# Attention and two gated layers on one core: v loaded head by head, block-diagonal q made ahead of k's high part, early weight pieces moved to other tiles

## The chip, the cores and the metric

The kernel runs on one core of one Trainium2 chip. The metric is the device time of one execution in microseconds (us); the median of several executions is compared. The engines are named as in the profile: PE (TensorE, matmul) with its weight loads PEld, ACT (ScalarE), DVE (VectorE), POOL (GpSimd) and SP (SyncE, which here only issues DMAs).

## The reference

Three stages follow each other. The attention has 4 batches of 8 heads, 1152 keys and head size 64; each pair of neighbouring queries is averaged first, so there are 576 queries a head.

```python
q_pool = q.reshape(B, H, S // 2, 2, D).mean(axis=3)
scores = scale * np.matmul(q_pool, k.transpose(0, 1, 3, 2))
scores = scores - np.max(scores, axis=-1, keepdims=True)
attn = np.exp(scores)
attn = attn / (np.sum(attn, axis=-1, keepdims=True) + 1e-09)
out = np.matmul(attn, v)
...
x = out.transpose(0, 2, 1, 3).reshape(B * S, H * D)      # 2304 x 512
h = x @ w_in;  x = (h - np.tanh(h)) @ w_out              # layer 1, d_ff 2048
h = x @ w2_in; x = (h / (1.0 + np.exp(-1.702 * h))) @ w2_out   # layer 2
```

The weights arrive as 64-bit floats, which the kernel reads as pairs of 32-bit integers.

## The kernel before

**Precision.** Every matmul operand is split into a high part that the matmul takes exactly (`qh`, `kh`, `vh`, `ph`) and a low part that is the rest (`ql`, `kl`, `vl`, `pl`), and a product is three matmuls (high by high, high by low, low by high). So each tensor costs a cast and a subtraction besides the matmuls: casts mostly on ACT, subtractions on DVE or POOL.

**Pairs and steps.** Two heads make a pair (16 pairs, numbered 0 to 15 here). A pair has 18 steps, i = 0 to 17: nine key blocks of 128 for each of its two heads. One step of the loop over `g` does, in this order: the scores of step g in two halves (four matmuls, L319 and L320), the exponentials `pf` and `ph` of each half on ACT (L321, L323), every second step a row-maximum tile for the pair that is next (`max_tile`: three matmuls L281 and a reduction on DVE, L284), `pl = pf - ph` of step g-1 (`rest`, L332; on POOL where i of that step is 2, 5, 8 or 11, else on DVE), and the six matmuls of probabilities by values of step g-3 (`pv`, L348). The scores have three PSUM buffers of half a step, the maximum tile has one. When a head's nine blocks are through, ACT copies the two halves of its sum out of PSUM (`u`, L354), which comes at i = 2 and i = 11.

**What is prepared for later pairs.** Each engine runs its instructions in program order, and the order is written by hand. `plan` gives, for the pair p+2 (or p+3), the step at which its pieces are emitted during pair p: `prep_qh` (ACT), `prep_kh` in two halves (ACT, L252), `prep_bdq` (ACT, two instructions, L247: q of the two heads laid out block-diagonally, the weights of the maximum tiles), `prep_ql` (DVE), `prep_kl` (POOL, L262), and the loads of q, k and v by SP. For the next pair n = p+1, `stack` at i = 2 and i = 13 issues six copies each from SP that lay out a head's operands (`a`, `q`), `max_rows` at i = 13 issues four more with the maxima (`q<-tt`), and `prep_v` at i = 3 and i = 12 makes `vh` and `vl` of one head on POOL (L301, L304).

**v.** `load_v` brings v of a whole pair, both heads, into the one buffer `vr` (576 KB) at i = 14. That buffer is last read by `prep_v` of the second head at i = 12, and the new contents are first read by `prep_v` at i = 3 of the next pair.

**Weights.** A weight piece is loaded (`ld`, L109, into one of two `raw` buffers) and then converted in three stages: stage 0 (ACT L122; DVE L123, L127), stage 1 (DVE L134, L138) and the split into high and low part (ACT L145, POOL L146). Layer 1's first eight pieces are spread over attention by the table `when`: kind ("i" for w_in, "o" for w_out), number, and then (pair relative to 16, step) of the load and of the three stages. Stages that the table does not name go into the first windows of layer 1. `split_x` at steps 13 to 16 of pair 15 splits the first block of the layer's input (cast on ACT L101, subtraction L102).

**Layers.** A window n of layer 1 or 2 is `h_part` (24 matmuls L552), the gate on ACT and DVE (`gate`), and two windows later `y_part` (L639). In layer 1 the gate's DVE instructions are L588, L594, L603, L606 and L608; jobs of weight conversion are run between L594 and L603.

Of the kernel before, what the change touches and what calls it, by code (L numbers as in the profile page):

```python
# [7 lines left out]
F32 = mybir.dt.float32  # L8
# [20 lines left out]
def tile_pooled_attention_two_moe(  # L29
# [14 lines left out]
    D = 64  # L44
# [141 lines left out]
    def attention(ctx: ExitStack):  # L186
# [34 lines left out]
        def load_v(p):  # L221
            vraw[p] = ap.tile([128, 2, KT, D], F32, tag="vr", name="vr")
            nc.sync.dma_start(out=vraw[p], in_=v[p // NPB, p % NPB])
# [19 lines left out]
        def prep_bdq(p):  # L243
            qs = pairs[p]["qs"]
            for s in range(2):
                r = slice(64 * s, 64 * s + 64)
                nc.scalar.activation(  # L247
                    bdqs[p % 2][r, :, r], qs[r, :].rearrange("p (j c) -> p j c", j=QJ), AF.Copy)
# [49 lines left out]
        def prep_v(p, s):  # L298
            vr = vraw[p]
            vh, vl = vt[(2 * p + s) % 3]  # L300
            nc.gpsimd.tensor_scalar(  # L301
                out=vh[:, :, 0:D], in0=vr[:, s], scalar1=1.0, scalar2=1.0,
                op0=ALU.mult, op1=ALU.mult)
            nc.gpsimd.tensor_tensor(  # L304
                vl[:, :, 0:D], vr[:, s], f32(vh[:, :, 0:D]), op=ALU.subtract)
# [84 lines left out]
        def normalise(p):  # L390
# [31 lines left out]
        for c in range(NKC):  # L422
            early.setdefault((NPAIR - 1, 13 + c), []).append(
                lambda c=c: split_x(0, [c], nc.gpsimd))
# [15 lines left out]
        load_v(0)  # L440
# [6 lines left out]
        with tc.tile_pool(name="ps_first", bufs=2, space=PSUM) as ps_first:  # L447
            for j in range(QJ):
                max_tile(0, j, ps_first)
                if j == 4:  # L450
                    prep_qh(1)
                    prep_kh(1, 0)
                    prep_kh(1, 1)
                    prep_bdq(1)
                    fill(2)
# [7 lines left out]
        load_v(1)  # L463
# [7 lines left out]
        for n in range(1, NPAIR):  # L471
# [4 lines left out]
            (2, 2): [(prep_qh,)], (2, 4): [(prep_kh, 0)], (2, 7): [(prep_kh, 1)],  # L476
            (2, 10): [(prep_bdq,)], (2, 14): [(prep_ql,), (load_v,)],
# [264 lines left out]
```

## Time and profile before

| | us |
|---|---|
| three runs | 1396.39, 1400.29, 1401.53 |
| median | 1400.29 |
| the profiled execution, its own time | 1398.61 |
| its span, first to last instruction | 1396.8 |
| PE busy in the span | 1316.1 (94%) |
| DVE busy | 1048.5 (75%) |
| ACT busy | 843.7 (60%) |
| POOL busy | 439.5 (31%) |

The span is 1.8 us shorter than the execution's own time. Busy shares are averages over attention and the two layers, which use the engines differently, so they do not tell what a step waits for; that is read from the timeline and the waits of the stretch in question.

### The profile page before, as it was taken

To read this page: it belongs to the slowest core of one execution; us is meant where nothing else is said; L and a number is where in the kernel's file an instruction comes from. 1 tells how busy PE (TensorE), PEld (TensorE's weight loads), DVE (VectorE), ACT (ScalarE), POOL (GpSimd) and SP (SyncE) were. 2 spreads that over 40 slices of the span, in tenths; PEclk is the share of its full clock that TensorE was granted. 3 is DMA by queue.
4 is the path that set the end of the run, shared out by engine and by line. 5 is a ranking of instruction groups with operands and counts; after the bars stand their busy time and mean duration, and the time that the engine had idled before them with its cause. 6 is when DMAs were issued, how large, how long until landed. Compare 5 with 4: busy or idle time off the path is not lost.

```text
span 1396.8 us, 20802 instructions
## 1 busy us (share of the span) xinstructions
PE 1316.1 (94%) x7632; PEld 1243.2 (89%) x7632; DVE 1048.5 (75%) x1230; ACT 843.7 (60%) x1885; POOL 439.5 (31%) x314
## 2 busy tenths in 40 slices
PE   4999999999999988899999999999999999999998
PEld 3999889998989887899899889899999999999997
DVE  5888887889898878898888888889963554645433
ACT  2798878988888776677656555656643422222211
POOL 6254444444445456233322332332310110110000
PEclk9899999999999999999999999999999999999999
DMA  7466666565667452111110110111110110110011
GB/s 191 123 173 165 154 146 164 148 162 141 165 149 174 102 122 83 58 46 31 46 46 31 42 35 31 46 46 31 46 60 31 46 46 31 52 39 31 24 46 68
DMA packets 44037, 117.70 MB, mean 84 GB/s; under 512 B 11936, under 2 KB 11936, under 8 KB 43936
## 3 DMA queue, kind: packets, MB, share of 16 engines
q1 hardware_dynamic: 43900, 116.38, 31.4%
q8 instruction: 60, 0.98, 0.3%
q14 instruction: 41, 0.34, 0.1%
q10 hardware_dynamic: 36, 0.00, 0.0%
HBM read 66.58 MB, written 4.79 MB: 51 GB/s over the span
## 4 chain that ended last, share of the span: by engine, by line
PE 47%; DVE 28%; ACT 9%; issue 5%; DMA 4%; POOL 3%; SPq 3%; DVEq 0%; POOLq 0%; ACTq 0%
PE y L639 14%; PE h L552 14%; PE pv L348 9%; PE mx L281 4%; DVE gg L606 3%; DVE gg L603 3%; PE sc L319 3%; DVE gg L608 3%; PE sc L320 3%; DVE d L594 3%; DMA vr<-in_v_dram 2%; ACT d L587 2%; DVE wt L123 2%; DVE wt L127 2%; DVE gg L588 2%
## 5 line engine op out<-in xcount | busy, mean ns | idle before, releaser
L321 ACT ACTIVATE pf<-sc 128x288 f32<-128x288 f32 x576 | 243.7, 425 | 75.8 <-PE sc L320 71.9
L323 ACT ACTIVATE ph<-sc 128x288 fp32r<-128x288 f32 x564 | 242.2, 429 | 0.0
L284 DVE TENSOR_REDUCE mt<-mx 128x1 fp32r<-128x1152 f32 x144 | 194.1, 1350 | 57.7 <-PE mx L281 57.4
L332 DVE TENSOR_TENSOR pl<-pf,ph 128x576 fp32r<-128x576 f32 x224 | 208.6, 953 | 6.9 <-ACT ph L323 6.0
L564 POOL TENSOR_TENSOR g<-gg,g 128x768 fp32r<-128x768 f32 x48 | 89.0, 1853 | 300.3 <-ACT g L562 281.0
L319 PE MATMUL sc<-q,a 128*128 128x288 f32 x576 | 169.2, 305 | 9.3 <-ACT pf L321 3.7
L320 PE MATMUL sc<-q,a 65*128 65x288 f32 x576 | 167.3, 303 | 2.6 <-DMA q<-tt 2.6
L612 ACT ACTIVATE a<-h 128x768 f32<-128x768 f32 x48 | 39.0, 812 | 214.5 <-PE h L552 214.5
L348 PE MATMUL pv<-pl,vh 128*128 128x288 f32 x576 | 140.3, 307 | 15.0 <-POOL pl L332 12.2
L652 DVE TENSOR_TENSOR xb<-xb,y 128x384 f32<-128x384 f32 (+1 forms) x126 | 73.0, 606 | 93.2 <-PE y L639 93.2
L348 PE MATMUL pv<-ph,vh 128*128 128x288 f32 x576 | 136.7, 301 | 3.9 <-ACT u L354 3.8
L348 PE MATMUL pv<-ph,vl 128*128 128x288 f32 x576 | 134.5, 297 | 0.0
L281 PE MATMUL mx<-kh,bdq 128*128 128x384 f32 x432 | 108.4, 362 | 24.4 <-DVE mt L284 16.8
L552 PE MATMUL h<-hl,w 128*128 128x384 f32 x720 | 130.5, 335 | 0.0
L332 POOL TENSOR_TENSOR pl<-pf,ph 128x576 fp32r<-128x576 f32 x64 | 107.3, 1676 | 65.3 <-ACT ph L323 55.3
L552 PEld LDWEIGHTS h<-hl,w 128*128 128x128 f32 x720 | 126.4, 188 | 1.2
L319 PEld LDWEIGHTS sc<-q,a 128*128 128x128 f32 x576 | 112.7, 196 | 16.2 <-ACT ph L323 9.9
L605 ACT ACTIVATE a<-u 128x768 f32<-128x768 f32 x48 | 40.7, 848 | 131.8 <-DVE gg L603 131.8
L348 PEld LDWEIGHTS pv<-pl,vh 128*128 128x128 f32 x576 | 96.6, 192 | 20.8 <-POOL pl L332 15.3
L320 PEld LDWEIGHTS sc<-q,a 65*128 65x128 f32 x576 | 111.6, 194 | 3.1 <-issue 3.1
L615 DVE TENSOR_TENSOR gg<-h,a 128x768 f32<-128x768 f32 x48 | 45.8, 955 | 84.8 <-ACT a L612 84.8
L348 PEld LDWEIGHTS pv<-ph,vh 128*128 128x128 f32 x576 | 102.5, 192 | 7.1 <-ACT u L354 6.9
(114 smaller groups left out, 2954.4 us busy)
## 6 DMA issues: line engine op xcount, KB each, us to landing
a<-kh SPq DMA_DIRECT2D x64, 288.0 KB
raw<-in_moe_w_in_dram SPq DMA_DIRECT2D x32, 512.0 KB
raw<-in_moe_w_out_dram SPq DMA_DIRECT2D x32, 512.0 KB
qr<-in_q_dram SPq DMA_DIRECT2D x16, 576.0 KB
kr<-in_k_dram SPq DMA_DIRECT2D x16, 576.0 KB
vr<-in_v_dram SPq DMA_DIRECT2D x16, 576.0 KB
q<-qh SPq DMA_DIRECT2D x64, 144.0 KB
a<-kl SPq DMA_DIRECT2D x32, 288.0 KB
```

What stands on the lines that cost most here:

```text
L281: nc.tensor.matmul(mx[:, a, 0:384], bdqs[p % 2][:, j, :], d["kh"][:, a * 384:(a + 1) * 384], start=True, stop=True)
L284: nc.vector.tensor_reduce(d["mt"][:, j:j + 1], mx[:, :, 0:384], AX.XY, ALU.max, negate=True)
L319: nc.tensor.matmul(sc, a1[:, ks], q2[:, xs], start=True, stop=False)
L320: nc.tensor.matmul(sc, a2[:, ks], q3[:, xs], start=False, stop=True)
L321: nc.scalar.activation(pf[:, xs], sc, AF.Exp, scale=SCALE)
L323: nc.scalar.activation(ph[:, xs], sc, AF.Exp, scale=SCALE)
L332: eng.tensor_tensor(pl, pf, f32(ph[:]), op=ALU.subtract)
L348: nc.tensor.matmul(accs[hd][x], w[:, t, :], r[:, x * HB:(x + 1) * HB], start=(t == 0 and n == 0), stop=(t == KT - 1 and n == 2))
L552: nc.tensor.matmul(hb[:, j, 0:TB], wi[:, c, w, :], x[r][c], start=(k == 0), stop=(k == 3 * NKC - 1))
L564: eng.tensor_tensor(gt[:, :, 1, :], g, f32(gt[:, :, 0, :]), op=ALU.subtract)
L639: nc.tensor.matmul(ys[m][:, 0:w], lhsT, rhs, start=(fp == 0 and k == 0), stop=(fp == 1 and k == 5))
L652: nc.vector.tensor_add(dst, dst, ys[m][:, 0:w])
```

## The change

v gets a buffer for each head of a pair (`vr0`, `vr1`, half the size each), with a load for each: the first head's at i = 6, the second's at i = 14. The block-diagonal q is emitted as two separate jobs at i = 4 and i = 5, and the halves of k's high part move from i = 4 and 7 to i = 6 and 8; `prep_ql` moves from i = 14 to i = 15. In the table `when` the loads and stages of the eight weight pieces get other steps, and all stages of piece ("o", 3) now stand in attention, so that none of them is left for layer 1. Two of the four subtractions of `split_x` for the first block go from POOL to DVE.

```diff
--- before.py
+++ after.py
@@ -218,9 +218,9 @@
             kraw[p] = ap.tile([128, S], F32, tag="kr", name="kr", bufs=2)
             nc.sync.dma_start(out=kraw[p], in_=k[p // NPB, p % NPB])
 
-        def load_v(p):
-            vraw[p] = ap.tile([128, 2, KT, D], F32, tag="vr", name="vr")
-            nc.sync.dma_start(out=vraw[p], in_=v[p // NPB, p % NPB])
+        def load_v(p, s):
+            vraw[p, s] = ap.tile([128, KT, D], F32, tag=f"vr{s}", name=f"vr{s}")
+            nc.sync.dma_start(out=vraw[p, s], in_=v[p // NPB, p % NPB][:, s])
 
         def prep_qs(p, eng=None):
             pairs[p] = dict(
@@ -240,12 +240,11 @@
             d = pairs[p]
             nc.vector.tensor_sub(d["ql"], d["qs"], f32(d["qh"][:]))
 
-        def prep_bdq(p):
-            qs = pairs[p]["qs"]
-            for s in range(2):
-                r = slice(64 * s, 64 * s + 64)
-                nc.scalar.activation(
-                    bdqs[p % 2][r, :, r], qs[r, :].rearrange("p (j c) -> p j c", j=QJ), AF.Copy)
+        def prep_bdq(p, s):
+            r = slice(64 * s, 64 * s + 64)
+            nc.scalar.activation(
+                bdqs[p % 2][r, :, r],
+                pairs[p]["qs"][r, :].rearrange("p (j c) -> p j c", j=QJ), AF.Copy)
 
         def prep_kh(p, x):
             xs = slice(x * SP, (x + 1) * SP)
@@ -296,13 +295,13 @@
                     queues[a].dma_start(out=row[:, :, a, :], in_=f32(tt[g:g + QJ, :]))
 
         def prep_v(p, s):
-            vr = vraw[p]
+            vr = vraw.pop((p, s))
             vh, vl = vt[(2 * p + s) % 3]
             nc.gpsimd.tensor_scalar(
-                out=vh[:, :, 0:D], in0=vr[:, s], scalar1=1.0, scalar2=1.0,
+                out=vh[:, :, 0:D], in0=vr, scalar1=1.0, scalar2=1.0,
                 op0=ALU.mult, op1=ALU.mult)
             nc.gpsimd.tensor_tensor(
-                vl[:, :, 0:D], vr[:, s], f32(vh[:, :, 0:D]), op=ALU.subtract)
+                vl[:, :, 0:D], vr, f32(vh[:, :, 0:D]), op=ALU.subtract)
 
         probs, accs, halves = {}, {}, {}
 
@@ -404,14 +403,14 @@
         pool_cast = range(NPAIR * NS - NS + 2, NPAIR * NS, 3)
         early = {}
         when = (
-            ("i", 0, (-8, 6), (-7, 5), (-7, 8), (-7, 16)),
-            ("i", 1, (-6, 6), (-5, 5), (-5, 8), (-5, 16)),
-            ("o", 0, (-4, 6), (-3, 5), (-3, 8), (-3, 16)),
-            ("i", 2, (-2, 2), (-2, 8), (-2, 11), (-2, 16)),
-            ("i", 3, (-2, 14), (-1, 4), (-1, 5), (-1, 7)),
-            ("o", 1, (-1, 0), (-1, 7), (-1, 8), (-1, 10)),
-            ("o", 2, (-1, 6), (-1, 11), (-1, 12), (-1, 14)),
-            ("o", 3, (-1, 9)),
+            ("i", 0, (-8, 6), (-7, 6), (-7, 14), (-6, 7)),
+            ("i", 1, (-6, 6), (-5, 6), (-5, 14), (-4, 7)),
+            ("o", 0, (-4, 6), (-3, 6), (-3, 14), (-2, 5)),
+            ("i", 2, (-2, 0), (-2, 6), (-2, 12), (-2, 14)),
+            ("i", 3, (-2, 4), (-2, 13), (-2, 15), (-2, 17)),
+            ("o", 1, (-2, 14), (-1, 1), (-1, 3), (-1, 5)),
+            ("o", 2, (-2, 16), (-1, 4), (-1, 6), (-1, 9)),
+            ("o", 3, (-1, 4), (-1, 8), (-1, 10), (-1, 12)),
         )
         ahead = []
         for kind, f, *steps in when:
@@ -421,7 +420,7 @@
             ahead += jobs[len(steps):]
         for c in range(NKC):
             early.setdefault((NPAIR - 1, 13 + c), []).append(
-                lambda c=c: split_x(0, [c], nc.gpsimd))
+                lambda c=c: split_x(0, [c], nc.gpsimd if c < 2 else nc.vector))
 
         load_q(0)
         load_k(0)
@@ -437,7 +436,8 @@
         prep_ql(0)
         load_q(1)
         load_k(1)
-        load_v(0)
+        load_v(0, 0)
+        load_v(0, 1)
         prep_kl(0, 0)
         prep_kl(0, 1)
         stack(0, 0)
...
         plan = {
-            (2, 2): [(prep_qh,)], (2, 4): [(prep_kh, 0)], (2, 7): [(prep_kh, 1)],
-            (2, 10): [(prep_bdq,)], (2, 14): [(prep_ql,), (load_v,)],
+            (2, 2): [(prep_qh,)], (2, 4): [(prep_bdq, 0)], (2, 5): [(prep_bdq, 1)],
+            (2, 6): [(prep_kh, 0), (load_v, 0)], (2, 8): [(prep_kh, 1)],
+            (2, 14): [(load_v, 1)], (2, 15): [(prep_ql,)],
             (2, 16): [(prep_kl, 0)], (2, 17): [(prep_kl, 1)], (3, 5): [(load_q,)],
             (3, 7): [(load_k,)], (3, 16): [(prep_qs,)],
         }
```

(In the part left out the two loads of v and the two jobs of block-diagonal q of the first pairs are written one after the other, where one call stood.)

**Block-diagonal q on ACT.** The rows show ACT in pair 1, around step 10 as it was: `bdq` after the last `ph` of step 10, then step 11's exponentials and the copies `u` of the finished head.

```order
L323 ACTIVATE ph<-sc 128x288
L247 ACTIVATE bdq_82<-qs 64x9x64 x2
L321 ACTIVATE pf<-sc 128x288
L323 ACTIVATE ph<-sc 128x288
L321 ACTIVATE pf<-sc 128x288
L323 ACTIVATE ph<-sc 128x288
L354 ACTIVATE u<-pv_786 128x288
L354 ACTIVATE u<-pv_787 128x288
```

In the change the same two instructions (now L245) stand in the same pair behind steps 4 and 5, and the first half of `kh` (now L251) behind step 6:

```order
L322 ACTIVATE ph<-sc 128x288
L245 ACTIVATE bdq_82<-qs 64x9x64
L320 ACTIVATE pf<-sc 128x288
L322 ACTIVATE ph<-sc 128x288
L320 ACTIVATE pf<-sc 128x288
L322 ACTIVATE ph<-sc 128x288
L245 ACTIVATE bdq_82<-qs 64x9x64
L320 ACTIVATE pf<-sc 128x288
L322 ACTIVATE ph<-sc 128x288
L320 ACTIVATE pf<-sc 128x288
L322 ACTIVATE ph<-sc 128x288
L251 ACTIVATE kh<-kr 128x576
```

Between step 10 and the copies `u` nothing but the exponentials is left on ACT.

**Loads of v in SP's queue.** The rows show SP around the turn from pair 7 to pair 8 as it was: the end of a `stack`, the load of v of a pair, the next `stack`, the sums `s`, then the loads of q, of weight piece ("i", 0) (`raw`) and of k.

```order
L275 DMA q_2_96<-ql 64x576
L223 DMA vr<-in_v_dram 128x1152
L270 DMA a_0_72<-kh 64x1152
...
L275 DMA q_0_90<-ql 64x576
L362 DMA s_4112<-u 64x1x9
L364 DMA s_4112<-u 64x1x9
L215 DMA qr<-in_q_dram 128x1152
L109 DMA raw<-in_moe_w_in_dram 128x1024
L219 DMA kr<-in_k_dram 128x1152
```

The same place in the change:

```order
L274 DMA q_2_96<-ql 64x576
L223 DMA vr_3926<-in_v_dram 128x576
L269 DMA a_0_72<-kh 64x1152
...
L274 DMA q_0_90<-ql 64x576
L361 DMA s_4132<-u 64x1x9
L363 DMA s_4132<-u 64x1x9
L215 DMA qr<-in_q_dram 128x1152
L223 DMA vr_4186<-in_v_dram 128x576
L109 DMA raw<-in_moe_w_in_dram 128x1024
L219 DMA kr<-in_k_dram 128x1152
```

Half of v (the second head's) is left where the whole load stood, and the other half (the first head's) stands between q and k.

**Weight loads at the turn to the last pair.** The rows show SP from the last `stack` (for pair 15) on, as it was: the loads of ("i", 3) and ("o", 1) follow it, those of ("o", 2) and ("o", 3) come later.

```order
L274 DMA a_1_91<-kh 64x1152
L275 DMA q_1_93<-ql 64x576
L109 DMA raw<-in_moe_w_in_dram 128x1024
L109 DMA raw<-in_moe_w_out_dram 128x1024
L362 DMA s_7391<-u 64x1x9
L364 DMA s_7391<-u 64x1x9
L109 DMA raw<-in_moe_w_out_dram 128x1024
```

In the change the loads of ("o", 1) and ("o", 2) follow that `stack`, and the load of ("i", 3) stands ahead of it, in step 4 of pair 14:

```order
L273 DMA a_1_91<-kh 64x1152
L274 DMA q_1_93<-ql 64x576
L109 DMA raw<-in_moe_w_out_dram 128x1024 x2
L361 DMA s_7441<-u 64x1x9
L363 DMA s_7441<-u 64x1x9
L109 DMA raw<-in_moe_w_out_dram 128x1024
```

On ACT the first stage (L122) that reads the first load after that `stack` stood behind step 4 of pair 15; the one that reads it in the change stands behind step 1.

## Rows read from the trace of the kernel before

**Rows 1.** Busy time by stretch: us, then PE, PEld, DVE, ACT, POOL.

```profile
126.40:159.00 32.60, 30.26 (x210) 28.97 (x209) 27.22 (x30) 27.34 (x81) 14.85 (x11) 1.00 0.63 151
...
287.40:318.00 30.60, 29.89 (x210) 28.90 (x209) 26.57 (x30) 27.38 (x81) 14.99 (x11) 1.00 0.68 178
318.00:351.10 33.10, 30.15 (x208) 28.87 (x208) 31.86 (x34) 28.19 (x82) 15.17 (x11) 1.00 0.61 148
...
517.50:556.20 38.70, 31.28 (x201) 28.39 (x200) 30.14 (x30) 26.60 (x78) 24.19 (x19) 0.96 0.38 102
```

**Rows 2.** Chain that ended last, pair 9: start us, us, what.

```profile
344.13 0.80 PE pv L348 x6
...
345.46 0.80 PE pv L348 x6
...
347.31 0.80 PE pv L348 x6
```

**Rows 3.** Waits of the whole run: us in total, times, longest us.

```profile
POOL vh L301 <- DMA vr<-in_v_dram: 25.5, 13, 3.5
...
PEld pv L348 <- POOL pl L332: 15.3, 14, 3.0
...
PEld sc L319 <- ACT ph L323: 9.9, 25, 1.4
...
PEld pv L348 <- ACT u L354: 6.9, 13, 0.6
```

**Rows 4.** Timeline of ACT in pair 8: start us, us, what, idle before it.

```profile
295.92 0.75 ACT L252 ACTIVATE kh<-kr 128x576 fp32r<-128x576 f32 x1
...
298.09 0.41 ACT L321 ACTIVATE pf<-sc 128x288 f32<-128x288 f32 x1 [0.21 <-PE sc L320]
...
305.76 1.38 ACT L247 ACTIVATE bdq<-qs 64x576 fp32r<-64x576 f32 x2
...
308.33 0.75 ACT L354 ACTIVATE u<-pv 128x288 f32<-128x288 f32 x2
```

**Rows 5.** Timeline of PE's weight loads in pair 8, those that waited.

```profile
294.34 0.19 PEld L319 LDWEIGHTS sc<-q,a 128*128 128x128 f32 x1 [0.37 <-ACT ph L323]
297.19 0.30 PEld L348 LDWEIGHTS pv<-pl,vh 128*128 128x128 f32 x2 [0.17 <-POOL pl L332]
307.91 0.19 PEld L319 LDWEIGHTS sc<-q,a 128*128 128x128 f32 x1 [0.42 <-ACT ph L323]
308.82 0.19 PEld L348 LDWEIGHTS pv<-ph,vh 128*128 128x128 f32 x1 [0.61 <-ACT u L354]
```

**Rows 6.** Chain that ended last, pair 3.

```profile
129.75 8.28 DMA vr<-in_v_dram
...
140.73 1.98 POOL pl L332
```

**Rows 7.** Pair 9: stage 1 in the timeline of DVE, and a wait of PE there.

```profile
338.14 0.69 DVE L138 SCALAR_TENSOR_TENSOR wt<-raw,wt 128x512 int32<-128x512 int32 x1
...
PE mx L281 <- DVE mt L284: 3.0, 3, 1.6
```

**Rows 8.** Timeline of SP and of ACT at the start of pair 15.

```profile
522.49 1.31 SPq L109 DMA_DIRECT2D raw<-in_moe_w_in_dram  x1
...
528.29 0.67 ACT L122 ACTIVATE wa<-raw 128x512 f32<-128x512 f32 x1 [2.81 <-DMA raw<-in_moe_w_in_dram]
```

**Rows 9.** Timeline of DVE and of POOL at the end of pair 15.

```profile
546.70 7.44 DVE L332 TENSOR_TENSOR pl<-pf,ph 128x576 fp32r<-128x576 f32 x5
...
552.00 1.53 POOL L102 TENSOR_TENSOR vl<-xb,vh 128x384 fp32r<-128x384 f32 x1
```

**Rows 10.** Timeline of DVE and of PE in the first windows of layer 1.

```profile
563.82 0.41 DVE L123 TENSOR_SCALAR wt<-raw 128x512 int32<-128x512 int32 x1
...
566.40 0.95 DVE L603 SCALAR_TENSOR_TENSOR gg<-a,gg 128x768 f32<-128x768 f32 x1
...
571.24 0.65 PE L639 MATMUL y<-g,w 128*128 128x384 f32 x1 [2.42 <-ACT g L562]
```

More of the change, by code (lines that the diff above doesn't have):

```diff
@@ L453, in attention @@
                     prep_kh(1, 1)
-                    prep_bdq(1)
+                    prep_bdq(1, 0)
+                    prep_bdq(1, 1)
                     fill(2)
@@ L462, in attention @@
         prep_kl(1, 1)
-        load_v(1)
+        load_v(1, 0)
+        load_v(1, 1)
         load_k(2)
```

## The prediction

> **What bounds the kernel now.** I read the table of stretches first, cut at the starts of the pairs (in the rows: pairs 3, 8, 9 and 15; the number behind POOL is the granted clock) [rows 1]. Attention is the part that the change touches, and PE is busy nearly all of the time there: 29.9 of 30.6 us in pair 8. But busy includes overlap, so the next view is the chain inside a quiet stretch [rows 2]. Three groups of six `pv` matmuls start at 344.13, 345.46 and 347.31: a step without a maximum tile takes 1.33 us, one with a tile 1.85, with nothing between. Nine of each make 28.6 us, the pair that PE could do without a wait. Pair 8 is 2.0 above it, pair 3 4.0, pair 9 4.5 [rows 1]. Pair 15 has no maximum tiles: 18 steps of 1.33, and 2.4 for the `pv` of the last three steps (three groups of 0.80, rows 2), are 26.3, and it takes 38.7. So what can be won or lost is PE's waits, and the waits of the whole run say on whom [rows 3]: `pv` on POOL's `pl` 15.3 us, scores on ACT's exponentials 9.9, `pv` on ACT's copies `u` 6.9. None of these engines is full; the waits come from what stands ahead in an engine's queue, and that is what the change edits. The sum below is made against the profiled execution, 1398.6 us of its own time (span 1396.8); the median of the runs shown, 1400.3, lies 1.7 above it, well inside the 5 us that the three runs span.
>
> **Block-diagonal q on ACT.** In pair 8 the two `bdq` take 1.38 us behind step 10's exponentials; they end at 307.14, and at 308.33, after four exponentials (so these take 1.2), come the copies `u` [rows 4]. PE pays twice: the scores of step 12 wait 0.42 us for an exponential to free a PSUM buffer, and the next head's first `pv` waits 0.61 for `u` [rows 5]. There are 13 waits on `u` in the run, 0.53 on average (6.9 / 13, rows 3); with 0.42 ahead of each, 13 x 0.95 = 12.4 us. With `bdq` gone from there, only `u` (0.75) is left. The other copies `u` of the pair, at step 2, have `qh` behind them, and both together cost PE one wait of 0.37 [rows 5].
>
> Does the stall come back at steps 4 to 8? Before, kh's first half (0.75) started at 295.92, and at 298.09 ACT was already waiting for scores again, 0.21 long [rows 4]. The first `bdq` (half of 1.38) takes the place of that half, so step 5's exponentials are no later. The second `bdq` and the moved half of kh then add 0.7 and 0.75 within two steps: less the 0.21, step 7 is some 1.1 late. Four exponentials need 1.2 of a step of 1.33 or 1.85, so 0.8 are given back every two steps, and three PSUM buffers let PE run one and a half steps ahead of ACT. By step 10 ACT is on time again. I take 12 us won; the bounds are 12.4 and 0 (the stall only moves).
>
> **v in two buffers.** POOL waits 25.5 us for v, in 13 waits [rows 3]. How PE feels it is seen in pair 3 [rows 6]: the load is issued at 129.75 and takes 8.28 us; `vh` and `vl` follow, and at 140.73 the `pl` that `pv` waits for. In the change the first head's half is issued at step 6, 15 steps ahead of its reader, some 24 us (15 x 1.6) against 8.3, and the second half 16 steps ahead. This wait disappears. Next in line is the `pl` behind `kl`, which costs PE 0.17 in pair 8 [rows 5]. The rest of the 15.3 us that `pv` waits for POOL's `pl` comes by the code's order from a weight split L146 queued at step 16 ahead of the second half of `kl`; these splits move to steps 5 and 7, where POOL has them behind one `pl` and well ahead of the next. I take 13 of the 15.3, with bounds 5 and 15.3. The extra load costs SP one more issue in each of 14 pairs (1.31 at most, as the load in rows 8), off PE's path as long as SP reaches step 13's copies in time.
>
> **Stage 1 of the early weight pieces.** In pair 9 DVE does L138, 0.69 us, with L134 of the same size ahead of it, in front of a maximum reduction, and PE's maximum tiles wait 3.0 us in that pair [rows 7]. Stage 1 moves from step 8 to step 14, where `prep_ql` makes room for it. Pair 11 has the same entry, and in pair 14 stage 1 moves behind the last maximum tile: 3 x 1.3 = 4 us won (bounds 0 and 6). Stage 0 keeps its place on DVE, since DVE has no other work in step 6, so its share of the 3.0 stays. On ACT it now meets `bdq` and kh, three times 0.3 or 0.4: 1 us lost.
>
> **The last pair.** The load issued at 522.49, directly behind the last `stack`, lands 5.8 us later, and ACT, which has reached its first stage, stands for 2.81 us [rows 8]. The change puts another load at the same place in SP's queue, but its first stage three steps earlier, 3 x 1.33 = 4.0. Nothing lets SP be earlier: the load stands behind ten copies of which the first waits for step 13's transposition. So ACT waits about 6.8 instead of 2.8, and behind it the exponentials of step 2, the subtractions and all of PE: 4 us lost. Against it stands the pair's end. Five `pl` on DVE take 7.44 us there, 1.49 each, while POOL runs one L102 after the other, 1.53 each [rows 9]: they go at POOL's pace. Two of four L102 leave POOL, and the stages end two steps earlier: 2 x 1.53 = 3 us won. Net 1 lost (bounds 6 won, 7 lost). The page "SBUF — State Buffer" of the Trainium skill (section "Who interferes with whom") says that a DVE instruction with two SBUF inputs and a GpSimd instruction that reads SBUF take the same port, and that one of them blocks until the other is through. Rows 9 agree; by that rule alone a subtraction moved from one engine to the other frees nothing, and the sum would be 3 us higher.
>
> **Start of layer 1.** Stages 0 and 1 of ("o", 3) stand on DVE from 563.82 until L603 starts at 566.40, 2.58 us in the middle of the first gate, and PE's first `y` waits 2.42 for that gate's end [rows 10]. The conversion is now in attention, its cast and split too. I take 4 us won: the 2.42, and 1.6 for what follows from it in the second window; bounds 1 and 6.
>
> **Sum.** 12 + 13 + 4 - 1 - 1 + 4 = 31 us; 1398.6 - 31 = 1367.6, said as 1367.
>
> **The rivals.**
> 1. *The last pair takes back more.* Not one but three loads, ("o", 1) to ("o", 3), come late, each by the 2.8 that the one costs now, and DVE and POOL never catch up: 9 more, 1376. For it: only four steps (5.3 us) lie between the last load and its first stage, less than the 5.8 seen. Against: SP's queue is short by then.
> 2. *`bdq` only moves the stall.* The 12 us fall away, 1379. For it: ACT's work in steps 2 to 8 grows by 1.4 us. Against: the starts followed above.
> 3. *POOL stays late without v.* `kl` still waits for the copies of `stack`, and `pl` follows it: 5 of 13 won, 1375.
> 4. *More comes free:* the stretches at the lower granted clock that lower pair 15's mean to 0.96 [rows 1] and its like, and the rest of DVE's waits in pairs 9 and 11: 12 more, 1355.
> 5. *Slower: SP's queue.* The extra half of v stands ahead of k, of the merge and of step 13's copies. If it held SP for its whole way, half of 8.28, then those copies, `kl` behind them and `pl` behind that would be late in 14 pairs: 14 x 4.1 = 58, so 1425. It decides the sign from 2.2 us a pair on (31 / 14). Against it: in pair 8 a weight load nearly as large as all of v already stands between q and k (SP's order, above), and that pair takes 30.6, the least of rows 1. The Trainium skill ("SBUF — State Buffer", "Summary: rules for kernel authors") speaks for this rival: a transfer that the DMA bounds should be one DMA and not several. No run so far shows it.
>
> **How the numbers follow.** Chances: the forecast 0.47, rival 1 0.15, rival 2 0.12, rival 3 0.08, rival 4 0.13, rival 5 0.05. The range 1353 to 1384 holds the forecast with the bounds of its terms and rivals 1 to 4; it leaves out rival 5, and two bad cases together. What can be told from no change is about 0.5%, 7 us. All cases but rival 5 end below 1393, and rival 5 may come in a weaker form that cancels the gain: faster 0.93, same 0.04, slower 0.03.
>
> **What would show it.** Right: no wait of POOL's `vh` on v; no waits of 0.6 on `u`; pairs 3 and 8 of equal length, about 29.5; ACT's first stage in pair 15 waiting 6 us or more for `raw`; the first `y` without a wait of 2.4. Wrong: scores waiting on ACT at steps 5 to 8 (rival 2); `pv` still waiting more than 8 us in all on POOL's `pl` (rival 3); a last pair above 42 us (rival 1); SP waiting on landings of v or k ahead of step 13's copies (rival 5).

## The result, and the profile after

The changed kernel takes 1375.7 us (median of four runs, 1374.27 to 1376.04); the kernel before 1398.34 (four runs). The ratio of the two is 0.984, with a 95% interval of 0.9805 to 0.9876. It is faster by 22.6 us by the medians and by 24.4 by the spans of the two profiled executions (1396.8 to 1372.4; the changed one, 1374.27, is the fastest of its four), where 31 were forecast.

Busy time by stretch, pairs 3, 8 and 15 of the changed kernel (us of the stretch, then PE, PEld, DVE, ACT, POOL, the granted clock, DMA share and GB/s), which answers to [rows 1]:

```profile
124.70:154.60 29.90, 29.51 (x210) 28.82 (x209) 26.83 (x30) 27.24 (x81) 16.28 (x11) 1.00 0.67 164
276.00:305.90 29.90, 29.53 (x210) 28.83 (x209) 26.73 (x30) 27.24 (x81) 16.40 (x11) 1.00 0.71 183
...
495.00:535.10 40.10, 31.51 (x200) 29.41 (x199) 32.12 (x35) 26.30 (x78) 22.14 (x17) 0.91 0.31 84
```

Pairs 3 and 8 are now equally long, as foretold (32.6 and 30.6 before), but 29.9 and not 29.5. Pair 15 is 1.4 longer. The waits of the whole run (us in total, times, longest), which answer to [rows 3]:

```profile
PEld mx L280 <- DVE mt L283: 30.0, 39, 5.8
...
PEld pv L347 <- DVE pl L331: 9.5, 21, 1.6
...
POOL vh L300 <- DMA vr<-in_v_dram: 3.8, 2, 2.4
PEld pv L347 <- POOL pl L331: 3.7, 6, 0.7
PEld sc L318 <- ACT ph L322: 2.8, 12, 0.4
```

The waits that the change was to remove are gone: `vh` for v 25.5 to 3.8, and none of that behind 64 us; `pv` for POOL's `pl` 15.3 to 3.7; scores for `ph` 9.9 to 2.8; the row for `u` (6.9) is no longer there. PE waits longer for DVE instead: its maximum tiles for the reduction L283, and `pv` for DVE's `pl`, some 5 us more each. The same two rows before:

```profile
PEld mx L281 <- DVE mt L284: 24.9, 25, 6.6
...
PEld pv L348 <- DVE pl L332: 4.5, 8, 1.7
```

**Where it went, step by step.** From the starts of the first score matmul of every step in PE's timeline I took each step's length, subtracted the 1.33 or 1.85 us that it needs (the prediction's figures), and added up pairs 1 to 13:

| excess over 1.33 or 1.85, us | step 4, 5 | step 7 | step 8, 9 | step 11 | step 12 | other steps | all |
|---|---|---|---|---|---|---|---|
| before | 11.7 | 1.0 | 15.9 | 4.5 | 11.0 | 2.6 | 46.7 |
| the change | 10.3 | 9.9 | 1.5 | 1.1 | 0.0 | 3.2 | 26.0 |

Step 12 is the stall behind `bdq`, steps 8 and 9 are the `pl` that POOL gave late for want of v. Both fell by about what was forecast. The steps 8 and 9 of pairs 4 and 13 are part of that, and there the wait cost clock too: the granted clock of these pairs was 0.95 and 0.90 before and is 1.00 in the change. Step 7 rose by 8.9, and that is most of what is missing from the forecast. Outside of these pairs, pair 0 (with what stands ahead of it) and pair 14 win 0.9 each, pair 15 loses 1.5, layer 1 wins 3.4 (428.2 to 424.8) and layer 2 nothing: 20.7 + 0.9 + 0.9 - 1.5 + 3.4 = 24.4.

**Step 7.** Pair 5 of the changed kernel, timeline of DVE, POOL and PEld (start us, us, engine, line, what, idle before it):

```profile
188.47 3.72 DVE L331 TENSOR_TENSOR pl<-pf,ph 128x576 fp32r<-128x576 f32 x2
...
194.05 2.52 DVE L396 TENSOR_TENSOR xb<-u,rb 128x384 f32<-128x384 f32 x2
196.49 1.34 DVE L283 TENSOR_REDUCE mt<-mx 128x1 fp32r<-128x1152 f32 x1
...
193.45 1.21 POOL L300 TENSOR_SCALAR vh<-vr 128x576 fp32r<-128x576 f32 x1
194.75 1.61 POOL L303 TENSOR_TENSOR vl<-vr,vh 128x576 fp32r<-128x576 f32 x1
196.32 1.52 POOL L331 TENSOR_TENSOR pl<-pf,ph 128x576 fp32r<-128x576 f32 x1
...
197.89 0.47 PEld L280 LDWEIGHTS mx<-kh,bdq 128*128 128x128 f32 x3 [1.16 <-DVE mt L283]
```

The two products that normalise a finished pair (L396, emitted at step 4) take 2.52 us; they end at 196.57, 0.21 behind the end of POOL's `vl` at 196.36. The reduction queued behind them ends at 197.83, and PE's next maximum tile has waited 1.16 for it. The same two products before the change, in the stretches of pairs 2 and 8, and after it, in the same pairs (us of the stretch, DVE's busy time in this line alone, instructions, granted clock, DMA share, GB/s):

```profile
93.90:124.50 30.60, 0.81 (x2) 1.00 0.65 161
...
287.40:318.00 30.60, 2.05 (x2) 1.00 0.68 178
```

```profile
93.80:124.70 30.90, 2.52 (x2) 1.00 0.64 159
...
276.00:305.90 29.90, 2.51 (x2) 1.00 0.71 183
```

Before, POOL often stood waiting for v just then (that was the 25.5 us), and DVE had the time to itself: the products took 0.81 or 0.82 in pairs 2, 3, 5, 6, 9 and 11. In the other seven they already lay beside work of POOL and took 2.02 to 3.26. With v there in time, `vh` and `vl` run at steps 4 and 5, beside the normalisation, and the products take 2.51 to 2.54 in every pair from 2 to 14. In pairs 3, 4, 7, 8 and 13, where DVE comes to them on time, that lengthens step 7 by 0.3 only; in the others DVE is late already (in pair 5 by the two `pl` of the first row above, 3.72 for both), and step 7 lasts 3.0 or more. The Trainium skill ("SBUF — State Buffer", "Who interferes with whom") says that a DVE instruction with two SBUF inputs and a GpSimd instruction that reads SBUF block each other until the first is through, and that a reduction does not take part in it on this chip; the rows agree, with L396 ending 0.21 us after `vl`, and L283, which reads PSUM here, at 1.34 us beside POOL's next `pl`.

**ACT in pair 8** (timeline; answers to [rows 4]):

```profile
284.29 0.74 ACT L245 ACTIVATE bdq<-qs 64x576 fp32r<-64x576 f32 x1
...
288.32 0.68 ACT L251 ACTIVATE kh<-kr 128x576 fp32r<-128x576 f32 x1
...
290.46 0.41 ACT L320 ACTIVATE pf<-sc 128x288 f32<-128x288 f32 x1 [0.25 <-POOL pl L331]
...
296.09 0.81 ACT L353 ACTIVATE u<-pv 128x288 f32<-128x288 f32 x2
```

ACT has caught up at 290.46, in step 8, where it waits for POOL: the moved `bdq` is absorbed within four steps, and nobody waits for `u`.

**The last pair and layer 1.** SP and ACT at the start of pair 15 (answers to [rows 8]), then DVE and PE in the first window of layer 1 (answers to [rows 10]):

```profile
498.79 2.03 SPq L109 DMA_DIRECT2D raw<-in_moe_w_out_dram  x2
...
503.87 0.67 ACT L122 ACTIVATE wa<-raw 128x512 f32<-128x512 f32 x1 [5.48 <-DMA raw<-in_moe_w_out_dram]
...
541.94 0.95 DVE L597 TENSOR_TENSOR d<-h,d 128x768 f32<-128x768 f32 x1
542.81 0.95 DVE L606 SCALAR_TENSOR_TENSOR gg<-a,gg 128x768 f32<-128x768 f32 x1
...
547.65 0.44 PE L642 MATMUL y<-g,w 128*128 128x384 f32 x1
```

ACT stands 5.48 us for the weight load (2.81 before, 6.8 forecast), and step 3 of the pair takes 7.96. Cut at its middle, the pair has lost and won: its first ten steps take 22.6 us (18.5 before), its last eight 17.5 (20.2 before).

L606 follows L597 at once, and the first `y` waits no longer (2.42 before). More hangs on that wait than its length. The stretch of `y` behind it, before and in the change (columns as in the first view):

```profile
573.20:578.40 5.20, 5.20 (x17) 5.20 (x18) 4.96 (x6) 3.64 (x6) 1.91 (x1) 0.53 0.70 223
```

```profile
549.60:554.80 5.20, 5.20 (x30) 5.20 (x31) 4.95 (x7) 4.40 (x8) 0.51 (x1) 1.00 0.70 243
```

Before, PE had stood 2.42 and then 1.31 us just ahead of it; the granted clock of TensorE was 0.53 (near the lower of its levels, 1.2 GHz), and PE ran 17 matmuls in 5.2 us. In the change only the second wait is left (1.52), the clock is 1.00 (2.4 GHz), and PE runs 30. The second window of layer 1 starts 18.6 us behind the first instead of 23.4; of these 4.8 us, 1.4 are lost again later in the layer.

### The profile page after: what moved, and what is told of

It is laid out like the page before. It is cut to its first block, busy times and chain, and to the rows that moved or that the text cites. A ratio compares the mean times of both kernels' runs of the same rounds, so it can differ in the third digit from the quotient of the medians.

```text
span 1372.4 us, 20838 instructions
## 1 busy us (share of the span) xinstructions
PE 1306.6 (95%) x7632; PEld 1238.9 (90%) x7632; DVE 1055.3 (77%) x1232; ACT 842.2 (61%) x1885; POOL 446.5 (33%) x312
## 4 chain that ended last, share of the span: by engine, by line
PE 28%; DVE 24%; ACT 5%; issue 3%; DVEq 0%; ACTq 0%
PE y L642 14%; PE h L555 14%; DVE gg L606 3%; DVE gg L609 3%; DVE gg L611 3%; DVE d L597 3%; ACT d L590 2%; DVE wt L123 2%; DVE gg L591 2%; DVE xb L655 2%; DVE wt L127 2%; DVE wt L134 2%; DVE wt L138 2%; ACT u L589 1%; ACT hl L101 1%
## 5 line engine op out<-in xcount | busy, mean ns | idle before, releaser
L283 DVE TENSOR_REDUCE mt<-mx 128x1 fp32r<-128x1152 f32 x144 | 194.2, 1351 | 39.1 <-PE mx L280 39.1
L318 PEld LDWEIGHTS sc<-q,a 128*128 128x128 f32 x576 | 111.7, 194 | 10.7 <-ACT pf L320 5.6
L555 PE MATMUL h<-hl,bdq 128*128 128x384 f32 x600 | 109.3, 337 | 0.0
L280 PEld LDWEIGHTS mx<-kh,bdq 128*128 128x128 f32 x432 | 75.1, 200 | 36.8 <-DVE mt L283 30.0
```

Source lines behind the costliest of these rows:

```text
L280: nc.tensor.matmul(mx[:, a, 0:384], bdqs[p % 2][:, j, :], d["kh"][:, a * 384:(a + 1) * 384], start=True, stop=True)
L283: nc.vector.tensor_reduce(d["mt"][:, j:j + 1], mx[:, :, 0:384], AX.XY, ALU.max, negate=True)
L318: nc.tensor.matmul(sc, a1[:, ks], q2[:, xs], start=True, stop=False)
L555: nc.tensor.matmul(hb[:, j, 0:TB], wi[:, c, w, :], x[r][c], start=(k == 0), stop=(k == 3 * NKC - 1))
```

## The experiments

Each was compared with the kernel before on its own chip (medians 1399.1 us for the parts alone and the normalisation at step 8; 1397.13 for the runs with block-diagonal q and v together, the normalisation at step 10, the later stages and the split on POOL; 1394.47 for the other four). As these medians differ by more than some of the effects, runs of different groups are compared by spans or by single steps. Expectations are quoted as they stood before each run. "Excess" is that of the table above.

### One part of the change alone

**Block-diagonal q alone** (in the kernel before; `prep_ql` goes to step 15 with it):

```diff
-            (2, 2): [(prep_qh,)], (2, 4): [(prep_kh, 0)], (2, 7): [(prep_kh, 1)],
-            (2, 10): [(prep_bdq,)], (2, 14): [(prep_ql,), (load_v,)],
+            (2, 2): [(prep_qh,)], (2, 4): [(prep_bdq, 0)], (2, 5): [(prep_bdq, 1)],
+            (2, 6): [(prep_kh, 0)], (2, 8): [(prep_kh, 1)],
+            (2, 14): [(load_v,)], (2, 15): [(prep_ql,)],
```

> The kernel before with only the block-diagonal q moved (one instruction each at steps 4 and 5, kh at 6 and 8, ql at 15). Theory of the prediction: 12 us less than before (1398 to about 1386), and no wait of 0.6 us of PE on the copies u is left in the quiet pairs. Rival (the stall only moves to steps 5 to 7): no change, 1396 to 1400, with waits of the scores on ACT there.

1386.43 us, ratio 0.9916 (0.9892 to 0.994): 12.7 won. The excess of step 12 goes from 11.0 to 0.0, and scores wait less for ACT (2.7 us from 64 to 517 us, 9.0 before): the rival that the stall only moves has fallen. But the 12.7 are not all of step 12. Steps 8 and 9 fall too, from 15.9 to 8.9, although v is loaded as before, and steps 5, 7 and 11 rise by 6.8 together.

**v in two buffers alone:**

```diff
-        def load_v(p):
-            vraw[p] = ap.tile([128, 2, KT, D], F32, tag="vr", name="vr")
+        def load_v(p, s):
+            vraw[p, s] = ap.tile([128, KT, D], F32, tag=f"vr{s}", name=f"vr{s}")
...
-            (2, 10): [(prep_bdq,)], (2, 14): [(prep_ql,), (load_v,)],
+            (2, 6): [(load_v, 0)],
+            (2, 10): [(prep_bdq,)], (2, 14): [(prep_ql,), (load_v, 1)],
```

> The kernel before with only v in two buffers and two loads. Port theory, made after the trace of the change: POOL no longer waits for v, but its vh and vl then run beside the two normalising multiplications on DVE (step 4), which take 2.5 us instead of 0.8 to 2.0, so that a maximum tile of step 7 waits for DVE up to 1.2 us; v alone wins only 5 to 8 us (1390 to 1393), and waits of maximum tiles on DVE at step 7 are seen although block-diagonal q is where it was. Rival (the new wait at step 7 comes from ACT's moved instructions): v alone wins the 10 to 13 us that were forecast (1385 to 1388), and no such wait shows.

1387.64 us, ratio 0.9923 (0.9897 to 0.9948): 11.5 won. Its waits from 64 to 517 us:

```profile
PEld mx L281 <- DVE mt L284: 17.9, 24, 1.8
...
PEld pv L348 <- ACT u L354: 6.1, 10, 0.6
```

The wait for `u` stays, as `bdq` is where it was. The excess of steps 8 and 9 falls from 15.9 to 1.3, and that of step 7 rises from 1.0 to 7.8: the new wait comes with the v part, not with ACT's moved instructions. In pair 5 the normalisation takes 2.52 us here too, and 0.81 in the kernel with `bdq` alone. The sum, though, is the rival's: 11.5, where the theory had 5 to 8. By the span it is 12.7, of which pairs 1 to 13 give 8.5 (the excess); pair 14 is 2.5 shorter, and pair 1 starts 1.5 earlier.

**The weight table and the split of the first block alone:**

```diff
-            ("i", 0, (-8, 6), (-7, 5), (-7, 8), (-7, 16)),
+            ("i", 0, (-8, 6), (-7, 6), (-7, 14), (-6, 7)),
...
-            ("o", 3, (-1, 9)),
+            ("o", 3, (-1, 4), (-1, 8), (-1, 10), (-1, 12)),
```

> The kernel before with only the table of the early weight pieces and the two subtractions on DVE. Theory: pairs 9 to 12 win about 7 us, pairs 13 and 14 some 2, the last pair loses 1 to 2 and the first windows of layer 1 win 3 to 4: 10 to 12 us less (1386 to 1388). Rival (v is what holds pairs 13 and 14, and the last pair's load takes the rest back): 5 us less or under, 1393 and above.

1390.17 us, ratio 0.9938 (0.9916 to 0.996): 8.9 won, where 10 to 12 were expected, and 5 or less by the rival. Layer 1 takes 424.8, as in the whole change, pair 15 takes 40.6. In pairs 3 and 5 step 8 keeps its 3.1 us, in pair 4 (34.2 before, 30.8 here) it does not: whether POOL's wait for v reaches PE hangs on small shifts.

**Block-diagonal q and v together** (the whole change, with the weight table and the split as they were):

> The changed kernel with the table of weight stages and the split of the first block as they were before, that is block-diagonal q and v alone. The three parts alone won 12.7, 11.5 and 8.9, which is 33, against 23 to 24 together. Theory (the loss is between the v part and the other two, because both remove the same waits in pairs 3 to 5 and 13, and then DVE is the limit): bdq and v together win 18 to 21, total about 1379, and the weights add only 3 to 5 to them. Rival (bdq and v are additive, and the weights lose their gain against them): 24, total about 1375, the same as the whole change.

1380.72 us, ratio 0.9878 (0.9858 to 0.9897): 16.4 won, less than the 18 to 21 expected, and far from the rival's 24. The three parts alone add up to 12.7 + 11.5 + 8.9 = 33.1, against 22.6 to 24.4 for the whole; v brings only 3.7 on top of `bdq` (16.4 less 12.7; 6.4 by the spans). The excess says why: steps 8 and 9, which v alone brings from 15.9 to 1.3, are at 8.9 with `bdq` alone and at 10.7 with the weight table alone, so that all three have won a part of the same wait. The weight part brings 5.1 on top of both by the spans (1377.5 to 1372.4), of it 3.8 at step 11 (excess 4.9 here, 1.1 in the whole change), the stage 1 that now stands later: 2.6 in pairs 9 and 11, 1.2 in pair 13.

### The wait at step 7

**The normalisation at step 8** (in the changed kernel):

```diff
-            if p > 1 and i == 4:
+            if p > 1 and i == 8:
```

> The change with one more edit: the two normalising multiplications on DVE stand at step 8 instead of step 4. Port theory: the waits of about 1.2 us of maximum tiles on DVE at step 7 (pairs 2, 5, 6, 9, 10, 11, 14) and of 0.3 (others) go, 8 to 10 us less than the change: 1366 to 1368. Rival (ACT's moved instructions make step 7 late): the waits stay and the time is that of the change, 1376 plus or minus 2. A third case: the multiplications make the same wait at step 9 or 11, also 1376, with the wait moved.

1378.58 us, ratio 0.986 (0.9836 to 0.9884): no gain. The excess of step 7 falls to 0.1, but that of step 11 rises to 13.8. Pair 5, DVE and PEld:

```profile
201.72 2.03 DVE L396 TENSOR_TENSOR xb<-u,rb 128x384 f32<-128x384 f32 x2
203.68 1.35 DVE L283 TENSOR_REDUCE mt<-mx 128x1 fp32r<-128x1152 f32 x1
...
205.07 0.47 PEld L280 LDWEIGHTS mx<-kh,bdq 128*128 128x128 f32 x3 [1.11 <-DVE mt L283]
```

There the products lie beside POOL's `pl` of step 8 and take 2.03, and the reduction behind them is late instead. In pairs 9, 11 and 13 it is DVE's `pl` ahead of them that lies beside POOL's and takes 1.98 or 1.99; the products take 0.76, and the reduction is late all the same.

**The normalisation at step 10:**

```diff
-            if p > 1 and i == 4:
+            if p > 1 and i == 10:
```

> The changed kernel with the normalisation of the finished pair (DVE, two instructions) emitted at step 10 instead of step 4. Theory (DVE is what is late next, since the normalisation and POOL's vh and vl now lie on top of each other at steps 4 and 5, and the maximum of step 7 comes behind both): at step 10 POOL has no v work, and DVE stood idle there for about 1.2 us, so the waits of the maximum tiles at step 7 (some 1.2 us in 7 pairs) go and no others come: 8 to 9 us less than the changed kernel, about 1367. Rival (DVE has simply too much in these pairs, wherever it stands): the wait reappears at step 11 as it did with the normalisation at step 8, about 1376 to 1379.

1369.41 us, ratio 0.9798 (0.9778 to 0.9818). POOL has no work there but in pairs 11 and 13, where the two products take 2.04; in the others they take 0.8, and DVE keeps time (pair 5, DVE):

```profile
200.05 1.36 DVE L283 TENSOR_REDUCE mt<-mx 128x1 fp32r<-128x1152 f32 x1 [0.26 <-PE mx L280]
201.33 0.75 DVE L331 TENSOR_TENSOR pl<-pf,ph 128x576 fp32r<-128x576 f32 x1
202.00 0.82 DVE L396 TENSOR_TENSOR xb<-u,rb 128x384 f32<-128x384 f32 x2
```

The excess of step 7 is 0.4 instead of 9.9. Pairs 1 to 13 take 5.4 us less than in the change, the span is 4.8 lower, the median 6.3. 8 to 9 were expected; the difference is that steps 8 to 13 now hold 6.5 of excess in all (2.6 without this edit), nearly all of it in pairs 9 to 13, most in 11 and 13. The rival (too much work on DVE wherever it stands) has fallen outside of pairs 11 and 13.

**v made later, the normalisation left at step 4.** This separates what DVE does from what POOL does beside it:

```diff
-                elif i == 3:
+                elif i == 6:
                     prep_v(n, 0)
```

> The changed kernel with POOL's vh and vl of the first head emitted at step 6 instead of step 3, and the normalisation left at step 4. Theory (DVE's two normalisations and POOL's vh and vl stretch each other when they lie on top of each other): apart, the normalisations take about 0.8 us instead of 2.5 for the two, the maximum waits at step 7 go, and the total comes to about 1369, like the kernel with the normalisation at step 10. Rival (the sum of DVE's work ahead of step 7 is what counts, not what POOL does): step 7 keeps its 3.04 in pairs 2, 5, 6, 9, 10, 11, total 1375 to 1377.

1370.51 us, ratio 0.9821 (0.9803 to 0.9839). It gives both answers within one run. First pair 5 (DVE, then POOL):

```profile
195.85 0.81 DVE L396 TENSOR_TENSOR xb<-u,rb 128x384 f32<-128x384 f32 x2
...
196.56 1.43 POOL L331 TENSOR_TENSOR pl<-pf,ph 128x576 fp32r<-128x576 f32 x1 [1.27 <-ACT ph L322]
```

and pair 3 (DVE, POOL, PEld):

```profile
132.99 3.29 DVE L396 TENSOR_TENSOR xb<-u,rb 128x384 f32<-128x384 f32 x2
...
132.41 1.95 POOL L331 TENSOR_TENSOR pl<-pf,ph 128x576 fp32r<-128x576 f32 x1
134.62 1.44 POOL L331 TENSOR_TENSOR pl<-pf,ph 128x576 fp32r<-128x576 f32 x1 [0.27 <-ACT ph L322]
...
137.60 0.47 PEld L280 LDWEIGHTS mx<-kh,bdq 128*128 128x128 f32 x3 [1.03 <-DVE mt L283]
```

In pair 5 the products fall into the 1.27 us in which POOL idles between two `pl`, take 0.81, and step 7 does not wait. In pair 3 POOL is at work through them (`kl` came late, and `pl` behind it), they take 3.29, and step 7 lasts 3.25. It is so in pairs 3, 4 and 13. In pairs 2, 5, 6 and four more it is as in pair 5 (pair 12's step 7 is 0.4 late), and in pairs 7, 8 and 9 the products take 2.05, which step 7 bears. The same instructions at the same place of DVE's program are fast or slow by what POOL does beside them. The rival (the sum of DVE's work alone) has fallen. The total expected, 1369, was not reached: the span is 3.3 lower than the change's, as three pairs keep the wait at step 7 and steps 8 and 9 go from 1.5 to 3.9.

### The last pair and layer 1

**Weight stages of the last pair later:**

```diff
-            ("o", 1, (-2, 14), (-1, 1), (-1, 3), (-1, 5)),
-            ("o", 2, (-2, 16), (-1, 4), (-1, 6), (-1, 9)),
-            ("o", 3, (-1, 4), (-1, 8), (-1, 10), (-1, 12)),
+            ("o", 1, (-2, 14), (-1, 6), (-1, 7), (-1, 8)),
+            ("o", 2, (-2, 16), (-1, 8), (-1, 9), (-1, 10)),
+            ("o", 3, (-1, 8), (-1, 12), (-1, 13), (-1, 14)),
```

> The changed kernel with the stages of the three weight pieces of the last pair some steps later (o1 at steps 6, 7, 8 instead of 1, 3, 5; o2 at 8, 9, 10 instead of 4, 6, 9; o3 loaded at 8, stages at 12, 13, 14). Theory (ACT's stand of 5.5 us for the late load at step 1 is what the last pair pays): the stand goes, pair 15 falls from 40.1 to about 36, the total by about 4, to 1371. Rival (the end of the pair, DVE and POOL at one pace, sets its length, so ACT's stand is hidden by what follows, or the later stages lengthen the end by as much): pair 15 stays at 39 to 41 and the total within 1 us of the changed kernel.

1370.61 us, ratio 0.9804 (0.9781 to 0.9827): pair 15 takes 36.7 instead of 40.1, close to the 36 expected. But 3.4 us is a difference of two larger ones. The two parts of the pair, in the change and here (columns as in the first view):

```profile
495.00:517.60 22.60, 16.77 (x102) 16.12 (x101) 17.53 (x20) 14.30 (x42) 10.82 (x8) 0.85 0.51 135
517.60:535.10 17.50, 14.74 (x100) 13.29 (x99) 14.59 (x16) 12.00 (x37) 11.32 (x10) 1.00 0.06 19
```

```profile
495.00:508.60 13.60, 13.60 (x101) 13.29 (x101) 11.91 (x15) 11.61 (x36) 8.04 (x7) 1.00 0.68 172
508.60:531.70 23.10, 17.64 (x100) 16.20 (x99) 18.41 (x21) 14.70 (x42) 13.43 (x11) 0.85 0.16 44
```

The first ten steps fall from 22.6 to 13.6, as ACT's stand is gone and the low granted clock with it. The last eight, into which the stages have moved, rise from 17.5 to 23.1, and the low clock is there now. So the theory holds for the stand, and the rival, that the later stages lengthen the end, is more than half right.

**All of the split on POOL:**

```diff
-                lambda c=c: split_x(0, [c], nc.gpsimd if c < 2 else nc.vector))
+                lambda c=c: split_x(0, [c], nc.gpsimd))
```

> The changed kernel with all four subtractions of the first block's split on POOL, as before. My term (two of them off POOL shorten the end of the last pair by 2 x 1.53): pair 15 becomes 3 us longer, total about 1378 to 1379. Rival (the two engines share a port there, so that a subtraction moved from one to the other frees nothing): no difference in pair 15, total within 1 us of the changed kernel.

1377.33 us, ratio 0.9854 (0.9834 to 0.9875); pair 15 takes 1.1 us longer than in the change (41.25 and 40.15 by the starts of its steps). It lies between my 3 and the rival's 0. DVE and POOL at the end of the pair:

```profile
530.41 4.53 DVE L331 TENSOR_TENSOR pl<-pf,ph 128x576 fp32r<-128x576 f32 x3 [1.55 <-POOL ph L324]
...
530.35 1.01 POOL L102 TENSOR_TENSOR vh<-xb,a 128x384 fp32r<-128x384 f32 x1
531.32 1.53 POOL L102 TENSOR_TENSOR vl<-xb,a 128x384 fp32r<-128x384 f32 x1
```

Beside L102 each `pl` of DVE again takes 1.51, as in [rows 9]; in the changed kernel, at the same place:

```profile
530.97 0.54 DVE L102 TENSOR_TENSOR vl<-xb,a 128x384 fp32r<-128x384 f32 x1
531.44 0.75 DVE L331 TENSOR_TENSOR pl<-pf,ph 128x576 fp32r<-128x576 f32 x1
```

So a subtraction that is moved from one engine to the other frees something: it takes 0.54 on DVE with POOL idle, and on POOL 1.01 where it starts ahead of DVE's `pl` (530.35 above) and 1.53 where it comes behind one. But it does not free all of the 1.53 either, as a part of that is the `pl` itself. What else the end of the pair waits for was not taken apart.

**Both edits, the normalisation at step 10 and the stages later** (the normalisation stays at step 4 in the last pair):

```diff
-            if p > 1 and i == 4:
+            if p > 1 and i == (10 if p < NPAIR - 1 else 4):
```

> The changed kernel with both edits that helped: the normalisation at step 10 (at step 4 in the last pair, which has no v to make), and the weight stages of the last pair later. If the two are independent, the last pair starts 5.1 us earlier (495.0 to 489.9) and is 3.4 us shorter: 8.5 us less than the changed kernel's 1375.7, about 1367, or 1365 by the medians of the two runs (6.3 and 5.1). Rival (the later stages fill up the last pair, and what is won ahead of it is lost at its end): 1369 to 1370.

1363.41 us, ratio 0.977 (0.9751 to 0.9789): the lowest median here, though the two kernels that follow lie within its interval. The two edits add up: pair 15 starts 4.7 us earlier and is 4.7 shorter than in the change, and the span is 9.6 lower, where 8.5 were expected.

**The same, with the stages of ("o", 3) left to layer 1:**

```diff
-            ("o", 3, (-1, 8), (-1, 12), (-1, 13), (-1, 14)),
+            ("o", 3, (-1, 8)),
```

> The same with piece (o, 3) only loaded in attention and its stages left to the first windows of layer 1, as before the change. My term (the conversion in the first gate costs layer 1 some 3.4 us): layer 1 becomes 3 to 4 us longer, the last pair 1 to 2 shorter, the total 1.5 to 2.5 above the kernel with both edits. Rival (the end of the last pair is where DVE and POOL are full, so the stages cost as much there): total within 0.7 us of it.

1365.24 us, ratio 0.9783 (0.9764 to 0.9801). Layer 1 takes 3.7 us more (424.6 to 428.3), and its first `y` waits again:

```profile
537.36 0.44 PE L642 MATMUL y<-g,w 128*128 128x384 f32 x1 [2.42 <-ACT g L565]
```

But the last pair is 2.5 shorter (35.4 to 32.9), so that the spans differ by 0.3 only and the medians by 1.8. The spans are those of one execution each, and the one profiled before (1364.6) lies 1.2 above its kernel's median, this one (1365.06) 0.2 below; so 1.8, as expected, is the better figure, though the ratios' intervals overlap. What is won in layer 1 by converting earlier is for the larger part paid in the last pair.

**Both edits, with the stages one or two steps earlier than there:**

```diff
-            ("o", 3, (-1, 8), (-1, 12), (-1, 13), (-1, 14)),
+            ("o", 3, (-1, 6), (-1, 10), (-1, 11), (-1, 12)),
```

> The kernel with both edits, with the weight stages of the last pair one or two steps earlier than there (o1 at 5, 6, 7; o2 at 7, 8, 9; o3 loaded at 6, stages at 10, 11, 12), still behind the landings. Theory (the end of the last pair is bound by DVE and POOL, so stages that are done before the block of the input is split shorten it): 1 to 2 us less. Rival (the work is the same and only moved): within 0.7 us.

1364.67 us, ratio 0.9776 (0.9758 to 0.9795), no gain: the last pair takes 35.5, as it did (35.4). The theory that earlier stages shorten it has fallen.

## Why the prediction was right, and where its sum was off

The direction, the places and most of the terms were right: 1375.7 lies in the range. The likeliest value, 1367, is 8.7 us too low, and one step accounts for most of that; the errors of the other terms nearly cancel, which is luck.

- **Block-diagonal q: right.** 12 forecast; 11.0 at step 12. That it wins 12.7 alone is partly chance, as steps 8 and 9 fall then too. The start of kh's first half was followed rightly: ACT has caught up at 290.46.
- **v: the wait was sized rightly, what follows it was not.** "This wait disappears" held, and 13 forecast stand against 14.4 at steps 8 and 9. The step that failed is the next: "Next in line is the `pl` behind `kl`, which costs PE 0.17". Next in line was DVE. In six of the thirteen pairs POOL's waiting had been time in which DVE's normalisation ran alone, in 0.81; with `vh` and `vl` brought into it, its two products take 2.5 in every pair, and step 7 cost PE 8.9 us more. The step followed POOL's own queue, and not who works beside POOL in the time in which it no longer waits. Moving either of the two away shows it: the normalisation to step 10 (step 7's excess 9.9 to 0.4), or v to step 6 (to 4.6, nearly all of it in the three pairs where POOL works beside it even so).
- **Stage 1 of the weight pieces: right in size, partly by luck.** 4 forecast, as 1.3 in each of pairs 9, 11 and 14; 3.8 at step 11, in the whole change against `bdq` and v. Pairs 9 and 11 give the 1.3 each, but the third is pair 13 with 1.2, which had the same entry and was not counted. Pair 14 is faster at step 11 too, by 1.6, and loses more at other steps (31.7 to 32.6 for the pair). As one sign of it I had named DVE's waits in pairs 9 and 11; their sum rose all the same, by step 7. The 1 us for ACT's meeting with `bdq` and kh cannot be told from other shifts.
- **The last pair: 1 forecast, 1.5 measured.** ACT's stand was 5.48 instead of 6.8, less than the 6 named as its sign; the first ten steps lose 4.1 (4 forecast), the last eight win 2.7 (3 forecast). Of that win, the split moved to DVE is 1.1 by pair 15, not 3. What the forecast had no term for is the granted clock behind ACT's stand: without the stand and the stages the first ten steps take 13.6 instead of 22.6.
- **Start of layer 1: 4 forecast, 3.4 measured over the layer.** "1.6 for what follows from it in the second window" was mostly the granted clock, 0.53 for 5.2 us behind the wait, which the forecast did not name. And I costed the conversion in its new place at nothing, without naming its cover, and it has none: without it the last pair is 2.5 shorter.
- **The sum.** 31 less the 8.9 of step 7 is 22.1; measured were 22.6 by the medians and 24.4 by the spans. The rest is small and of both signs: by the spans -1.0 for `bdq`, +1.4 for v, -0.6 for stage 1 (4.5 to 1.1 at step 11), -0.5 for the last pair, -0.6 for layer 1, +1.0 for the loss on ACT that does not show, and what had no term: +1.4 at steps 4 and 5, -0.6 at the other steps, +0.9 each in pairs 0 and 14.

Of the rivals, the second fell with the first experiment. The first (three loads late, 1376) has the right total by luck: only one load stands in the way, in 5.48 us, and pair 15 is at 40.1, not above the 42 named as its sign. The third has no sign either, with 3.7 us for POOL's `pl`. The fourth did not come: DVE's waits grew, and pair 15's mean clock fell from 0.96 to 0.91; even the kernel with both edits, at 1363.41, is short of its 1355. The fifth: the extra load costs nothing that shows, pairs 3 and 8 being shorter than before.

What stays open: what the 10.3 us of excess are that the table still shows at steps 4 and 5; and whether the weight stages of pairs 9 to 15 can be placed so that neither end of the last pair waits for them. That was tried only in the last pair.

## What to carry to other kernels

When a wait is taken away, ask not only who is next in that engine's queue, but which engine has been working undisturbed while it lasted. DVE work with two SBUF inputs that must be in time (here the products ahead of a reduction that PE waits for) belongs where POOL idles: 0.8 us there and up to 3.3 beside its work. Work that is moved out of a bound stretch has to be priced in the place to which it goes: in the last pair, moving stages won 9.0 us in one half and lost 5.6 in the other. And a wait of PE is to be read with the granted clock of the stretch behind it.

## What the runs showed of the hardware

How far it goes was not expected: the same two products (128x384 and 128x192) on DVE took 0.8 us with POOL idle and 2.03, 2.52 or 3.29 beside its work, while the reductions from PSUM took 1.29 to 1.36 in every run.

The granted clock of TensorE fell behind ACT's stand in pair 15. Three stretches of the changed kernel, the columns as in the first view:

```profile
497.70:504.30 6.60, 1.85 (x14) 1.62 (x13) 1.66 (x3) 1.12 (x4) 0.03 (x1) 1.00 0.97 261
504.30:511.10 6.80, 6.21 (x25) 6.11 (x26) 6.70 (x11) 5.36 (x17) 2.81 (x2) 0.50 0.23 70
511.10:517.00 5.90, 5.41 (x41) 5.18 (x40) 5.87 (x6) 4.53 (x14) 5.80 (x4) 1.00 0.13 47
```

PE was busy for 1.85 of 6.6 us, and then had 1.2 GHz instead of 2.4 for 6.8 us, in which it ran 25 matmuls; in the next 5.9 us it ran 41. With the stages moved later there is no such stretch at this place, but one of the same length near the pair's end (523.6 to 530.4), so not all of the clock's cost was won back: the pair's mean is 0.91 in both.
